# Fewer unread matmuls before chunk 0, and batch 2's first transposes at the end of chunk 0

## The chip, the cores and the metric

The kernel runs on one core of one Trainium2 chip (trn2). The core has five engines that follow their own instruction streams: TensorE (PE in the profile; its weight loads are PEld), VectorE (DVE), ScalarE (ACT), GpSimd (POOL) and SyncE (SP). The metric is the device time in microseconds (us), as the median of several executions. For the kernel before it is 323.74 us, the median of five (322.66 to 325.79).

## The reference

Two layers follow each other: sliding-window causal attention over 64 positions, and a mixer whose token mixing is of low rank, followed by an MLP.

```python
# q, k, v: (8, 8, 576, 64)
scores = scale * np.matmul(q, k.transpose(0, 1, 3, 2))
mask = (rel >= 0) & (rel < 64)            # rel = query position - key position
attn = softmax(np.where(mask, scores, -1e9))
x = np.matmul(attn, v)                    # heads side by side: (8, 576, 512)
h = x.transpose(0, 2, 1) @ U @ V          # U (576, 32), V (32, 576)
u = x + h.transpose(0, 2, 1)
out = u + np.maximum(u @ w_ch1, 0.0) @ w_ch2   # 512 -> 2048 -> 512
```

## The kernel before

The 8 x 576 = 4608 tokens of the MLP are cut into nine chunks of 512 (`NCH`). A chunk needs attention and token mixing of its tokens first. A batch has 576 tokens, so chunk c of the MLP runs beside the attention of batch b = c + 1. Batch 0's attention stands alone in front of chunk 0.

The order of the work is written out by hand. `mlp(c)` gives a list of pieces that feed TensorE: 16 pieces `ch1(i)` (each four matmuls of 128x512 into a PSUM tile `psA`, L602, then a relu to `c1_i` on ScalarE, L613, or VectorE, L611) and 16 pieces `ch2(t, r)` (four matmuls into `psU`, L644; after the fourth quarter VectorE adds `u`, L653, into `osb`, which SP writes out). In chunk 0 the second half is ordered so that t = 0, 1, 2 advance together and t = 3 comes last. These 32 pieces are slots 0 to 31. The attention's pieces are put into slots by tables: `PLACE_1` for batch 1, `PLACE_2` for batch 2, `PLACE` for the later ones. A slot runs its MLP piece and then the pieces placed there; in chunk 0 after slot 20 the placed pieces come first. Instructions of one engine run in the order in which they are recorded.

The pieces of a batch are:

- `KT` (four for batches 0 to 2): VectorE transposes the raw keys and queries, L239, in the order keys 0, queries 0, keys 1, queries 1. They write `kt` and `qt`, of which there is one each. The raw data come by GpSimd's DMAs, `load_kq` (L105 for batches 0 to 2, L114 later); values by `load_v`, L126 and L130.
- `S` (six): scores in PSUM (`sc`, L345; for batch 0 L286 and L303), ScalarE's exp to `pts` (L353), and VectorE's product with the mask (L360). For a paired batch, the first two of the six need only keys 0 and queries 0.
- `VC`: copies of the values, shifted by 64 rows (L138, L139).
- `PV` (five): weights times values into `xr` (L382), the reciprocal of the row sums (L391) and the scaled result `xs` (L401).
- `U`, then `V` (three): token mixing. `V` makes `psv` (L453) and VectorE adds it to `xs`, giving `un` (L464), two tiles at a time. For batches 0 and 1, `XT` (L498) and `UP` (L512) make the transposed `uTc` directly in PSUM, which is copied out at L521.

PSUM tiles of two kinds matter here: the pool `ps_big` has two buffers, which `sc`, `xr`, `psv`, `xT` of batch 1 and the unread tiles take in turn; the pool `ps_mm` has three, which `psA` and `psU` take in turn.

`turn_over(n, cols)` (L698) issues n matmuls on a tile of zeros, whose results nobody reads. They keep TensorE busy while it has nothing else: 56 of 128 columns and 50 of 64 before batch 0's first scores, ten of 64 between its second and third score piece, one of 128 before and after its PV piece 3, and a few more before chunk 0. Each of them is two instructions, a weight load and a matmul.

For chunk 1 the tables give: slot 0 has `V` of batch 1 (first pair of tiles) and the transposes of keys 0 and queries 0 of batch 2, slot 1 the second pair of `V`, slot 2 keys 1, slot 3 queries 1 and the first two score pieces, slot 6 the next two, slot 8 the last two, slot 11 the first two PV pieces.

Of the kernel before, what the change touches and what calls it, by code (L numbers as in the profile page):

```python
# [16 lines left out]
def kernel(  # L17
# [12 lines left out]
    B, H, S, D = q.shape  # L30
# [3 lines left out]
    P = nc.NUM_PARTITIONS  # L34
    W = 64
# [63 lines left out]
    def load_kq(b):  # L99
        r = RUN[b]  # L100
        for part in range(NJ if PAIRED[b] else 4):
            for x, src in (("k", k), ("q", q)):
                dst = raw[x, b % 2]
                if PAIRED[b]:
                    nc.gpsimd.dma_start(  # L105
                        out=dst[:, part * RD : (part + 1) * RD],
                        in_=src[b, part * NQ : (part + 1) * NQ].rearrange(
                            "i (p c) d -> (i p) (c d)", c=RP
                        ),
                    )  # L110
                    continue
                m, dh = divmod(part, 2)
                off = 32 * (1 - dh)
                nc.gpsimd.dma_start(  # L114
                    out=dst[32 * part : 32 * (part + 1), off : off + NJJ * RD].rearrange(
                        "p (n x) -> p n x", x=r * D
                    ),
                    in_=src[b, m * NJJ : (m + 1) * NJJ].rearrange(
                        "h (m p e) d -> p (h m) (e d)", p=32, e=r
                    ),  # L120
                )

    def load_v(b):
        va, vb = vA[b % 2], vB[b % 2]
        for t in range(NFULL):
            nc.gpsimd.dma_start(  # L126
                out=va[:, t, :, 0:D],
                in_=v[b, :, t * P : (t + 1) * P, :].rearrange("h p d -> p h d"),
            )
        nc.gpsimd.dma_start(  # L130
            out=vb[0:W, NFULL, :, 0:D],
            in_=v[b, :, NFULL * P : S, :].rearrange("h p d -> p h d"),
        )
# [401 lines left out]
    def TR(g):  # L535
        def f():
            c, t = divmod(g, TPC)
            if c not in stages:
                stages[c] = stg_pool.tile([P, 4 * NDC, TPC, 32], BF16, name="stg")
            nc.vector.transpose(  # L540
                out=stages[c][:, :, t, :],
                in_=u_tiles[g].rearrange("p (j x) -> p j x", x=32),
            )

        return f

    def next_loads(c):
        def f():
            for i, j in last_pieces[c + 1]:
                rows = slice(32 * j, 32 * (j + 1))  # L550
                nc.gpsimd.tensor_copy(
                    out=hold[rows, 0:1], in_=uT_of(c + 1)[rows, 0, i * TPC * 32 : i * TPC * 32 + 1]
                )
            load_kq(c + 3)

        return f

    def gather(c):
        def f():
            run = TPC * 32  # L560
            queues = (nc.sync, nc.scalar, nc.gpsimd)
            done = {}
            for n in range(16):
                i, j = (n + n // 4) % 4, n % 4
                done[n % 3] = (i, j)
                queues[n % 3].dma_start(  # L566
                    out=uT_of(c)[32 * j : 32 * (j + 1), :, i * run : (i + 1) * run],
                    in_=stages[c][32 * i : 32 * (i + 1)].rearrange(
                        "p (d j) t q -> p d j (t q)", j=4
                    )[:, :, j, :],  # L570
                )
            last_pieces[c] = (done[0], done[1])

        return f

        return f

    def mlp(c):
# [102 lines left out]
    }  # L681
    PLACE_2 = {
        "V1": [0, 1, 17],
        "KT": [0, 0, 2, 3],
        "S": [3, 3, 6, 6, 8, 8],
        "VC": [7],
        "PV": [11, 11, 13, 13, 15],
        "U": [16],
        "V": [18, 19, 21],
    }  # L690
# [7 lines left out]
    def turn_over(n, cols=CH, to=None):  # L698
        for _ in range(n):
            nc.tensor.matmul(  # L700
                (unread if to is None else to)[:, 0, 0:cols],
                idle[:, 0:P],
                idle[:, 0:cols],
                start=to is None,
                stop=to is None,
            )

    def fresh():
        return ps_big.tile([P, 2, CH], FP32, name="unread", tag="big")

    unread = fresh()
    turn_over(56, P)
    turn_over(50, W)
    att = {0: attention(0, alone=True)}
    a = att[0]
    for f in a["KT"]:
        f()
    a["S"][0]()
    a["S"][1]()
    turn_over(10, W)  # L720
    a["S"][2]()
    for f in a["VC"][0:2]:
        f()
# [16 lines left out]
    xT0 = [psum["x0"].tile([P, 2, CH], FP32, name=f"xT{i}", tag="x0") for i in range(2)]  # L740
    unread = xT0[0]
    a["PV"][2]()
    turn_over(1, P)
    a["PV"][3]()
    turn_over(1, P)
    a["PV"][4]()
    a["XT"][0]()
    turn_over(2, P, xT0[0])
# [17 lines left out]
    for c in range(NCH):  # L766
        slots = [[] for _ in range(NSLOT + 1)]

        def place(b, parts, where):
            if b not in att:  # L770
                att[b] = attention(b)
            for part in parts:
                for f, s in zip(att[b][part], where[part]):
                    slots[s].append(f)

        b = c + 1
        if b == 1:
            for f, n in zip(att[0]["V"], (6, 8, 10)):
                slots[n].append(f)
        if b < B:  # L780
            if b == 1:
                load_kq(2)
            if b + 1 < B:
                load_v(b + 1)
            if b == 1:
                slots[23].append(lambda: load_kq(3))
            where = {1: PLACE_1, 2: PLACE_2}.get(b, PLACE)
            if b == 2:
                place(1, ("V",), {"V": where["V1"]})
            if b <= 2:  # L790
                place(b, ("KT",), where)
            place(b, ("VC", "S", "PV"), where)
            if 3 <= b + 1 < B:
                place(b + 1, ("KT",), {"KT": KT_LATE[b]} if b in KT_LATE else PLACE)
            place(b, ("U", "XT", "UP") if b == 1 else ("U", "V"), where)
        if 2 <= c + 1 < NCH:
            g0 = (b * S) // P
            first = (c + 1) * TPC
            last = max(first + t - g0 for t in range(TPC)) // 2 if b < B else 0
            ready = where["V"][last] if b < B else 18  # L800
            for t in range(TPC):
                slots[ready - 1 + t // 2 if t < TPC - 1 else ready + 1].append(TR(first + t))
            slots[ready + 1].append(gather(c + 1))
            if c > 0 and c + 3 < B:
                slots[ready + 1].append(next_loads(c))
        for n, (fill, extra) in enumerate(zip(mlp(c) + [lambda: None], slots)):
            early = c == 0 and n > 20
            for f in extra + [fill] if early else [fill] + extra:
                f()
# [30 lines left out]
```

## Time and profile before

| what | value |
|---|---|
| median of five executions | 323.74 us (322.66 to 325.79) |
| the profiled execution: device time | 324.57 us |
| the profiled execution: span from first to last instruction | 322.9 us |
| mean granted TensorE clock | 0.982 of full speed |
| VectorE busy | 208.9 us |
| ScalarE busy | 106.9 us |
| L602 psA, 576 matmuls | 132.8 us, 380 ns each |
| L644 psU, 560 matmuls | 127.2 us, 379 ns each |
| chunk 0 begins (first psA) | 24.96 us |

How to read it: a line of a timeline gives the start, the duration, the engine, the line of the kernel, the operation, out<-in, the tile's shape, and how many were merged; brackets at the end give the idle time of the engine before it and what ended it. [...]512-column matmuls shown with 380 ns follow each other every 216 ns; distances are better taken from start to start. A line of the stretches gives, for a window, each engine's busy time with its count of instructions, then the granted TensorE clock, the DMA share (outstanding packets over 16 engines, so it can pass 1) and GB/s.

### The profile page before, as it was taken

What the parts mean: (1) busy time and instruction counts of PE and PEld (TensorE: products, weight loads), DVE (VectorE), ACT (ScalarE), POOL (GpSimd) and SP (SyncE); (2) the same over time, 40 slices, a digit from 0 to 9 for tenths busy, and PEclk for the clock granted to TensorE, in tenths of its full rate; (3) what the DMA queues carried; (4) which work ended last, traced back from release to release, by engine and by line L of the source; (5) the groups of instructions that cost most, each with busy time, mean ns of one, the idle gap of its engine ahead of it and who ended that gap; (6) DMA issues with size and microseconds to landing.
All of it is one profiled execution on the core that took longest, in us unless ns stands there. A gap on an engine that the chain in (4) does not pass through costs nothing.

```text
span 322.9 us, 7092 instructions
## 1 busy us (share of the span) xinstructions
PE 313.3 (97%) x2929; PEld 154.0 (48%) x2929; DVE 208.9 (65%) x366; ACT 106.9 (33%) x174; POOL 105.1 (33%) x156
## 2 busy tenths in 40 slices
PE   7799999989999999999999999999999999999995
PEld 7474454545444544454444444444444444444444
DVE  7544968478698759777957795879578722412211
ACT  1535363265205520552046303730273004203400
POOL 8672428541038403751394036512000200030000
PEclk9859999999999999999999999999999999999999
DMA  7999999999639993899999929995500150050011
GB/s 119 160 196 208 206 124 149 210 194 135 20 94 181 173 116 85 157 165 136 90 186 195 116 37 181 195 145 30 181 0 2 32 164 1 2 163 32 2 67 65
DMA packets 108929, 38.05 MB, mean 118 GB/s; under 512 B 98352, under 2 KB 101808, under 8 KB 108896
## 3 DMA queue, kind: packets, MB, share of 16 engines
q0 software_dynamic: 92480, 25.63, 107.1%
q1 hardware_dynamic: 11232, 10.69, 9.9%
q10 hardware_dynamic: 5184, 1.28, 1.8%
q8 instruction: 23, 0.38, 0.5%
q14 instruction: 10, 0.08, 0.1%
HBM read 48.94 MB, written 9.44 MB: 181 GB/s over the span
## 4 chain that ended last, share of the span: by engine, by line
PE 88%; DMA 6%; DVE 3%; issue 1%; POOL 0%; DVEq 0%; POOLq 0%
PE psU L644 37%; PE psA L602 36%; PE xr L382 4%; DMA vA<-in_v_dram 4%; PE sc L345 3%; DMA qr<-in_q_dram 2%; PE psv L453 2%; DVE un L464 1%; PE psU L626 1%; PE xT L498 1%; PE pshh L434 1%; PE xT L512 1%; PE sc L303 1%; DVE qt L239 1%; PE sc L286 1%
## 5 line engine op out<-in xcount | busy, mean ns | idle before, releaser
L602 PE MATMUL psA<-uTc,w1b 128*128 128x512 bf16 x576 | 132.8, 380 | 0.1
L644 PE MATMUL psU<-w2b,c 128*128 128x512 bf16 x560 | 127.2, 379 | 0.0
L613 ACT ACTIVATE c<-psA 128x512 bf16<-128x512 f32 x101 | 60.3, 597 | 171.0 <-PE psA L602 170.7
L644 PEld LDWEIGHTS <-c 128*128 128x128 bf16 x560 | 53.5, 98 | 63.9 <-issue 1.5
L602 PEld LDWEIGHTS <-w1b 128*128 128x128 bf16 x576 | 53.5, 98 | 61.7 <-issue 0.3
L566 POOL DMA_DIRECT2D uTc<-stg x35 | 19.2, 556 | 117.5 <-DVE stg L540 78.5
L653 DVE TENSOR_TENSOR osb<-psU,un 128x512 f32<-128x512 f32 x35 | 23.5, 671 | 33.6 <-PE psU L644 33.5
L611 DVE TENSOR_SCALAR c<-psA 128x512 bf16<-128x512 f32 x43 | 29.5, 687 | 22.4 <-PE psA L602 20.8
L126 POOL DMA_DIRECT2D vA<-in_v_dram x32 | 28.5, 893 | 28.2 <-PE psA L602 12.6
L360 DVE TENSOR_TENSOR pts<-pts,mask 128x768 bf16<-128x768 bf16 x42 | 22.8, 556 | 17.9 <-ACT pts L353 15.8
L353 ACT ACTIVATE pts<-sc 128x768 bf16<-128x768 f32 x42 | 31.8, 810 | 3.9 <-PE sc L345 3.9
L464 DVE TENSOR_TENSOR un<-psv,xs 128x512 bf16<-128x512 f32 (+1 forms) x40 | 26.0, 675 | 10.8 <-PE psv L453 10.6
L401 DVE TENSOR_TENSOR xs<-xr,rcp 128x512 bf16<-128x512 f32 (+1 forms) x39 | 26.9, 691 | 1.3
L382 PEld LDWEIGHTS <-pts 128*64 128x64 bf16 x576 | 13.4, 116 | 10.5 <-DVE xs L401 5.1
L540 DVE STREAM_TRANSPOSE stg<-un 128x512 bf16<-128x512 bf16 x28 | 18.4, 683 | 0.0
L114 POOL DMA_DIRECT2D kr<-in_k_dram x20 | 16.7, 837 | 3.6 <-DMA vA<-in_v_dram 2.1
L247 DVE STREAM_TRANSPOSE qt<-qr 128x576 bf16<-128x576 bf16 x20 | 15.8, 788 | 3.2 <-DMA vA<-in_v_dram 3.2
L114 POOL DMA_DIRECT2D qr<-in_q_dram x20 | 16.8, 841 | 1.8 <-DMA vA<-in_v_dram 1.0
L382 PE MATMUL xr<-vB,pts 128*64 128x65 bf16 x320 | 16.6, 202 | 0.2 <-issue 0.2
L247 DVE STREAM_TRANSPOSE kt<-kr 128x576 bf16<-128x576 bf16 x20 | 15.7, 786 | 1.2 <-DMA kr<-in_k_dram 1.2
L345 PEld LDWEIGHTS <-kt 64*64 64x64 bf16 (+1 forms) x720 | 10.2, 106 | 10.8 <-issue 9.1
L345 PE MATMUL sc<-qt,kt 64*64 64x128 bf16 (+4 forms) x720 | 13.3, 215 | 1.5 <-DVE qt L239 0.7
(70 smaller groups left out, 165.4 us busy)
## 6 DMA issues: line engine op xcount, KB each, us to landing
out_dram<-osb SPq DMA_DIRECT2D x35, 256.0 KB, 2.2
kr<-in_k_dram POOLq DMA_DIRECT2D x26, 288.0 KB, 10.8
qr<-in_q_dram POOLq DMA_DIRECT2D x26, 288.0 KB, 12.0
vA<-in_v_dram POOLq DMA_DIRECT2D x32, 128.0 KB, 13.3
w2b<-in_moe_w_ch_dram POOLq DMA_DIRECT2D x2, 1024.0 KB, 19.7
uTc<-stg SPq DMA_DIRECT2D x42, 32.0 KB, 2.3
uTc<-stg ACTq DMA_DIRECT2D x35, 32.0 KB, 2.3
uTc<-stg POOLq DMA_DIRECT2D x35, 32.0 KB, 2.0
```

The lines of the kernel that those rows point to most:

```text
L114: nc.gpsimd.dma_start(out=dst[32 * part : 32 * (part + 1), off : off + NJJ * RD].rearrange("p (n x) -> p n x", x=r * D), in_=src[b, m * NJ ...
L126: nc.gpsimd.dma_start(out=va[:, t, :, 0:D], in_=v[b, :, t * P : (t + 1) * P, :].rearrange("h p d -> p h d"),)
L247: nc.vector.transpose(out=dst[:, n * S : (n + 1) * S].rearrange("q (m p e) -> q m e p", p=32, e=r), in_=src[:, 32 + n * RD : 32 + (n + 1) ...
L345: nc.tensor.matmul(sc[half * W : (half + 1) * W, g, (a - lo) * W : (z - lo) * W], operand("k", g, jj, e, kb * W, (kb + 1) * W), operand("q ...
L353: nc.scalar.activation(out=dst, in_=sc[:, :, 0 : PB * W].rearrange("p g (n w) -> p g n w", w=W), func=ACT.Exp, scale=scale,)
L382: nc.tensor.matmul(xr[r0 : r0 + W, h // 4, (h % 4) * VW : (h % 4 + 1) * VW], pts[:, g, jj * NB + blk, :], rhs, start=True, stop=True,)
L401: nc.vector.tensor_tensor(out=x[lo:hi, t, :, :].rearrange("p (a h) d -> p a h d", a=2), in0=xv[:, :, :, 0:D], in1=rcp[lo:hi].to_broadcast( ...
L464: nc.vector.tensor_tensor(out=u_tiles[g][rs, :], in0=ps[rs, n, :], in1=xt[n][rs], op=ALU.add)
L602: nc.tensor.matmul(to if c < 2 else to.rearrange("p (t i q) -> p t i q", i=4, t=TPC), w1b[:, dc, n * P : (n + 1) * P], uT_cols(dc), start= ...
L611: nc.vector.tensor_relu(out=c1[i][:], in_=ps)
L613: nc.scalar.activation(out=c1[i][:], in_=ps, func=ACT.Relu)
L644: nc.tensor.matmul(acc[t][:], c1[i][:, t * P : (t + 1) * P], w2b[:, i, :], start=(i == 0), stop=(i == NFC - 1),)
```

## The change

It changes three things. The unread matmuls: 74 of 156 columns instead of 56 of 128 and 50 of 64 in front; two of 512 columns instead of ten of 64 between score pieces; the two single ones between PV pieces are dropped. Batch 2's transposes of keys 0 and queries 0 move from slot 0 of chunk 1 to slots 30 and 31 of chunk 0, where they stand ahead of those slots' MLP pieces. Batch 2's last two score pieces move from slot 8 to slot 9.

```diff
     PLACE_2 = {
         "V1": [0, 1, 17],
-        "KT": [0, 0, 2, 3],
-        "S": [3, 3, 6, 6, 8, 8],
+        "KT0": [30, 31],
+        "KT": [2, 3],
+        "S": [3, 3, 6, 6, 9, 9],
...
     unread = fresh()
-    turn_over(56, P)
-    turn_over(50, W)
+    turn_over(74, 156)
...
-    turn_over(10, W)
+    turn_over(2)
...
     a["PV"][2]()
-    turn_over(1, P)
     a["PV"][3]()
-    turn_over(1, P)
     a["PV"][4]()
...
-            if b <= 2:
-                place(b, ("KT",), where)
+            if b == 1:
+                place(1, ("KT",), where)
+            if b == 2:
+                att[2]["KT"] = att[2]["KT"][2:]
+                place(2, ("KT",), where)
             place(b, ("VC", "S", "PV"), where)
+            if b == 1:
+                place(2, ("KT",), {"KT": PLACE_2["KT0"]})
```

P is 128, W is 64, and `turn_over` without a width uses 512 columns.

## Prediction

> **What bounds the kernel now.** I read the page first: its engine shares, the clock row and the chain that ended last.
>
> ```profile
> PE 313.3 (97%) x2929; PEld 154.0 (48%) x2929; DVE 208.9 (65%) x366; ACT 106.9 (33%) x174; POOL 105.1 (33%) x156
> PEclk9859999999999999999999999999999999999999
> q8 instruction: 23, 0.38, 0.5%
> PE 88%; DMA 6%; DVE 3%; issue 1%; POOL 0%; DVEq 0%; POOLq 0%
> ```
>
> TensorE carries the span, and the chain is TensorE in nearly every stage. So only two things are worth anything: TensorE's own work, and the holes between its matmuls. After chunk 0 begins (24.96 us) the waits of TensorE list very few holes, so I went to its timeline for chunk 1:
>
> ```profile
> 40.12 0.76 PE L345 MATMUL sc<-qt,kt 32*64 32x128 bf16 x48
> 40.81 1.90 PE L644 MATMUL psU<-w2b,c 128*128 128x512 bf16 x8
> ...
> 64.05 1.89 PE L602 MATMUL psA<-uTc,w1b 128*128 128x512 bf16 x8
> 66.66 0.54 PE L345 MATMUL sc<-qt,kt 32*64 32x128 bf16 x24 [0.72 <-DVE qt L239]
> 67.77 0.54 PE L345 MATMUL sc<-qt,kt 32*64 32x128 bf16 x24 [0.57 <-DVE un L464]
> 68.25 2.76 PE L602 MATMUL psA<-uTc,w1b 128*128 128x512 bf16 x12
> 70.94 0.82 PE L345 MATMUL sc<-qt,kt 32*64 32x128 bf16 x56
> 71.69 1.90 PE L602 MATMUL psA<-uTc,w1b 128*128 128x512 bf16 x8
> 73.52 0.64 PE L345 MATMUL sc<-qt,kt 32*64 32x64 bf16 x43
> 74.41 0.37 PE L345 MATMUL sc<-qt,kt 32*64 32x128 bf16 x13 [0.24 <-issue]
> ```
>
> Three holes stand in ten microseconds. The first waits for a transpose of batch 2's queries, the second for VectorE to free a PSUM buffer (`un`, L464), and the third for nothing that the profile shows ("issue"). VectorE in the same stretch says why:
>
> ```profile
> 59.07 1.29 DVE L521 CAST uTc<-xT 128x512 bf16<-128x512 f32 x2 [2.91 <-PE xT L512]
> 61.66 0.69 DVE L653 TENSOR_TENSOR osb<-psU,un 128x512 f32<-128x512 f32 x1 [1.30 <-PE psU L644]
> 62.96 1.40 DVE L464 TENSOR_TENSOR un<-psv,xs 64x512 bf16<-64x512 f32 x2 [0.60 <-PE psv L453]
> 64.27 1.25 DVE L239 STREAM_TRANSPOSE kt<-kr 128x576 uint32<-128x576 uint32 x1
> 65.36 1.24 DVE L239 STREAM_TRANSPOSE qt<-qr 128x576 uint32<-128x576 uint32 x1
> 66.44 1.28 DVE L464 TENSOR_TENSOR un<-psv,xs 128x512 bf16<-128x512 f32 x2
> ```
>
> It is idle for 1.30 and 0.60 us before chunk 1, and then has six things to do in a row while TensorE waits for the fourth and the last.
>
> **Part 1: two transposes to the end of chunk 0.** I measure by starts[...]. Eight psA matmuls followed by scores take 73.52 - 71.69 = 1.83 us, so the first scores could start at 64.05 + 1.83 = 65.88. A pair of score pieces of 48 matmuls needs 40.81 - 40.12 = 0.69 us, so psA could go on at 66.57. It goes on at 68.25. The two holes cost 1.68 us.
>
> Where do the two transposes go? After the casts of L521, in the idle stretch. With the pitches of the rows (1.20 for a pair of L521 or L464, 1.09 and 1.08 for the transposes, 0.6 for osb): casts 59.07 to 60.27, kt from there, qt from 61.36 (ends 62.6), osb at 62.44 instead of 61.66, the first `un` pair at 63.1, the second at 64.4, ended 65.7. Their raw data landed long before: the last packets of the two loads of L105 (issued 45.86 and 47.18) at 50.85 and 52.22. They write the single kt and qt tiles, whose last readers, batch 1's scores, are through at 46.9.
>
> What is queued behind them? The osb add, 0.8 us later, frees the psU bank that chunk 1's third psA piece takes (start 64.05): freed at 63.1, 0.9 us to spare. Its output DMA on SP goes as much later, with three more osb buffers and nobody waiting. The second `un` pair frees the buffer for the second score piece: 65.7 against 65.88 + 0.35 = 66.2, 0.5 us to spare. The other two transposes then run 65.6 to 67.9, and the next score piece needs them at 66.57 + 2.69 = 69.3. No DMA is moved, and POOL's queue is not passed. So this part gives **-1.68**; the cover that makes the move free is VectorE's idle time of 1.9 us, and without it the two transposes (2.2 us) would only change places.
>
> **Part 2: last scores one piece later (8 to 9).** The same 56 matmuls, so no work on TensorE. But ScalarE now has c_9's relu ahead of their exps. With the rows' exps (0.75 each in a pair) and mask products (0.6), the last product ends about 75.4 while TensorE reaches the second PV piece, its reader, at about 75.5 (77.47 + 0.32 less 1.68 and the 0.44 of part 3). In before 0.7 us lay between. Bounds: 0 and 0.3. I take **+0.1**.
>
> **Part 3: 42 fewer unread matmuls.** I counted TensorE's instructions in the built program and paired them one to one with the trace's 2929 weight loads and 2929 matmuls. Two stalls with the "issue" mark are true stalls: at 18.91 us, instruction 706, and at 74.41, instruction 1986. They are 1280 = 5 x 256 apart. So I read 706 + 256k as the block borders. The trace's records of the instruction queue (the page's q8, 23 packets of 16 KB) fit: packets landed at 17.37 and 72.80, and TensorE went on 1.54 and 1.61 us later. The second stall costs (74.71 - 73.52) - (71.69 - 70.94) = 0.44 us.
>
> Here a rule speaks against the change. The Trainium skill, "Runtime: NRT & Kernel Launch", section "Instruction fetch mechanics", says that instructions come in blocks of 256, fetched ahead, and that the cost of a border is "mostly hidden". By the rule, moving borders is worth 0 and the whole change gives -1.6; by the row it is worth up to 0.44 at each of two borders. The rows decide: at 20 of 22 borders the rule holds, and at two, where the block before is full of short matmuls, it fails.
>
> The change takes out 84 instructions (118 unread matmuls become 76, each with a weight load), so the borders fall on old instructions 790 + 256k. The border at 18.91 moves to the UP matmuls (0.2 to 0.4 us each, 22.7 to 24.4), where the block has 3 us more. Its stall was worth little: the next PV piece waits until 18.93 for `xs` of PV 2 (VectorE, ended 18.90) anyhow. Without the stall and the two unread matmuls between PV pieces, I get that piece at about 19.0 instead of 19.33. But the last U matmul follows the last `xs` (21.00, matmul 21.07), and VectorE's chain of rcp 0.24 and xs 0.69 ends that one only 0.24 earlier. The granted clock there is half:
>
> ```profile
> 14.00:14.50 0.50, 0.50 (x31) 0.49 (x32) 0.00 (x0) 0.50 (x1) 0.32 (x1) 0.67 1.81 173
> 24.00:24.50 0.50, 0.50 (x4) 0.23 (x3) 0.00 (x0) 0.30 (x1) 0.12 (x1) 0.59 1.08 205
> ```
>
> It falls near 14.17 and returns near 24.41, by the clock and not by the work, so 0.24 gained before is filled with half-speed matmuls: **-0.12** (between 0 and -0.35).
>
> The border at 74.41 moves to the start of the second PV piece, and the one before it to old instruction 1814, in the middle of the third and fourth score pieces: 71.2 less 1.68 = 69.5. From there to the new border at about 75.7 is 6.2 us. How long does a block need from the crossing of the border before? Crossing 14.01, usable 18.91: 4.9 us. Crossing 67.97, usable 74.41: 6.4 us. The next packet (asked for at 74.41) landed at 81.59, so usable about 83.1: 8.7 us. The DMA share rises from 1.83 to 2.57 and 4.31 in those stretches (68 to 72, 72 to 76, 76 to 80). Bounds for the new stall: 0 and 2.5. The nearest row is the second, 1.5 us earlier in the kernel: 6.4 - 6.2 = 0.2; with the rising load I take 0.3. So this border gives -0.44 + 0.3 = **-0.14**.
>
> The warm-up itself is free: 74 matmuls of 156 columns, 130 ns each until 3.93 us and 67 after (from 107 and 56 ns at 128 columns), end at 7.55 instead of 7.11, and the first scores wait for qt until 8.45. The two of 512 columns (0.43 for 0.29) lie before the wait until 12.22 for the second qt, whose data comes by DMA.
>
> **Sum.** -1.68 + 0.1 - 0.12 - 0.14 = -1.84, made against the profiled execution: 324.57 (span 322.9 and 1.7 around it) becomes 322.7. That execution lies 0.83 above the median of the five, 323.74, which becomes 321.9. Later stages keep the gain: the loads of L114 and L126 follow TensorE's progress (POOL waits for psA), and batch 3's raw data landed by 80.1 with its first transpose at 92.12.
>
> **Rivals.**
> *The block arrives late (slower).* The fetch asked for at 69.5 meets batch 2 and 3's loads as the one of 74.41 did, takes 8.7 us or a little more, and TensorE stops 2.5 us or more before the second PV piece. From a fetch of 8.3 us on (6.2 + 2.14, all other gains) the kernel is slower. For it: the DMA share of 4.31. Against: the fetch of 67.97 lies nearer. Time: 323.74 - 2.14 + 2.6 = 324.2. Chance 0.10.
> *The gain is not passed on.* A later wait stands at a fixed time. For it: a hole of 0.37 at 188.18, behind loads that took 13.07 us. Against: those loads start on TensorE's progress. It would leave stage 0 and a part: 323.3. Chance 0.13.
> *The clock moves.* "TensorE: Matmul & The Clock Gate", section "Part 1: The HAM clock gate", says that the clock falls only after an idle window of about 3.4 us[...]; the trace differs, it fell after a hole of 1.62 us (10.6 to 12.22). By the rule the change's denser filler gives 0. By the row the start is near a limit. If the half clock did not come, 16 matmuls of XT and 4 of UP would save 16 x 51 + 4 x 210 ns = 1.7 us, with the rest some 2.5: 319.4. Chance 0.07. Longer half speed into chunk 0 would cost half of its length; it shares the slow side's remainder.
> *The likeliest*, 0.70: 320.9 to 322.9 by itself.
>
> **How the numbers follow.** A measurement of this kernel can tell about 0.5% (1.6 us) from no change. The forecast 321.9 is 0.57% below 323.74, hence close to that line: of its 0.70 some 0.43 lies below 322.1, 0.24 within, and 0.03 is left for a longer half speed (slower); clock 0.07 faster; not passed on 0.13 same; late block 0.05 within, 0.05 slower. So faster 0.50, same 0.42, slower 0.08. The range 320.5 to 323.7 leaves out the clock case and most of the late block.
>
> **What would show it.** Right: the first two score pieces of chunk 1 start near 65.9 and 66.2 and psA follows at 66.6, without the marks of qt and un; the transposes stand at 60.3 and 61.4 on VectorE with osb behind them; no issue mark inside a score pair of chunk 1. Wrong: a new hole of TensorE at 62 to 65 (osb's bank), an issue mark of over 0.5 us at the second PV piece near 75.7, PV waiting for the mask product, or other times at which the clock falls and returns; these would void parts 1, 3, 2 and the sum's base in turn.

## The result and the profile after

The changed kernel takes 322.91 us as the median of 43 executions, the kernel before 324.56 us as the median of 80 in the same measurements (its first five had 323.74). These medians lie 1.65 us apart. The ratio on record leaves out slow executions, those over 1.5% above the fastest of the same kernel (five of the changed kernel's): it is 0.9934 with a 95% interval of 0.9918 to 0.9950, 0.66% or 2.1 us faster. The forecast ratio was 0.9943. The profiled execution has 323.18 us with a span of 321.5, against 324.57 and 322.9, so that pair shows 1.4 us.

From the page of the changed kernel:

```profile
PE 313.0 (97%) x2887; PEld 154.4 (48%) x2887; DVE 208.6 (65%) x366; ACT 106.7 (33%) x174; POOL 104.5 (33%) x156
PEclk9959999999999999999999999999999999999999
PE 58%; DMA 22%; DVE 7%; POOL 5%; issue 4%; SPq 3%; ACT 1%; DVEq 0%; POOLq 0%; ACTq 0%
```

TensorE is as busy as before. The chain's shares look very different, but that is no new bound: it is followed back from the end through whatever released each step, and where it now takes the loads, those themselves start on TensorE's progress. Chunks 2 to 8 have the same lengths as before within 0.6 us. TensorE's timeline shows what did move:

```profile
14.29 0.19 PE L382 MATMUL xr<-vB,pts 128*64 128x65 bf16 x1
15.54 0.19 PE L382 MATMUL xr<-vA,pts 128*64 128x65 bf16 x1 [1.06 <-issue]
...
45.67 0.75 PE L345 MATMUL sc<-qt,kt 32*64 32x64 bf16 x51
47.05 0.25 PE L345 MATMUL sc<-qt,kt 32*64 32x128 bf16 x5 [0.64 <-issue]
47.23 1.04 PE L644 MATMUL psU<-w2b,c 128*128 128x512 bf16 x4
...
64.49 1.89 PE L602 MATMUL psA<-uTc,w1b 128*128 128x512 bf16 x8
66.31 0.76 PE L345 MATMUL sc<-qt,kt 32*64 32x128 bf16 x48
67.00 2.76 PE L602 MATMUL psA<-uTc,w1b 128*128 128x512 bf16 x12
69.69 0.82 PE L345 MATMUL sc<-qt,kt 32*64 32x128 bf16 x56
70.44 2.76 PE L602 MATMUL psA<-uTc,w1b 128*128 128x512 bf16 x12
73.13 0.79 PE L345 MATMUL sc<-qt,kt 32*64 32x64 bf16 x56
```

In chunk 1 all three holes are closed: from the psA matmuls at 64.49 to those at 67.00 are 2.51 us, where before 68.25 - 64.05 = 4.20 were needed. But two "issue" stalls stand at places that had none before: 1.06 us in batch 0's first PV piece, and 0.64 us inside batch 1's last score pair in chunk 0, which before ran through:

```profile
46.09 0.78 PE L345 MATMUL sc<-qt,kt 32*64 32x64 bf16 x56
46.80 1.04 PE L644 MATMUL psU<-w2b,c 128*128 128x512 bf16 x4
```

VectorE after the change, in the stretch of the moved transposes:

```profile
59.51 1.29 DVE L521 CAST uTc<-xT 128x512 bf16<-128x512 f32 x2 [2.91 <-PE xT L512]
60.71 1.25 DVE L239 STREAM_TRANSPOSE kt<-kr 128x576 uint32<-128x576 uint32 x1
61.80 1.24 DVE L239 STREAM_TRANSPOSE qt<-qr 128x576 uint32<-128x576 uint32 x1
62.88 0.68 DVE L653 TENSOR_TENSOR osb<-psU,un 128x512 f32<-128x512 f32 x1
63.60 2.59 DVE L464 TENSOR_TENSOR un<-psv,xs 64x512 bf16<-64x512 f32 x4
```

They fill the idle time, the add waits for them, and the four `un` follow without a break. TensorE shows no wait for the late osb.

By stages, measured between the first psA weight loads of the chunks in the profiled executions (us; the kernels in the lower rows are those of the experiments below):

| kernel | first stage | chunk 0 | chunk 1 | chunks 2 to 6 | ratio to before (95%) |
|---|---|---|---|---|---|
| before | 24.91 | 36.34 | 36.92 | 165.5 | 1 |
| changed | 24.50 | 37.19 | 34.77 | 165.9 | 0.9934 (0.9918 to 0.9950) |
| place_only | 24.41 | 36.34 | 34.77 | 165.4 | 0.9926 (0.9896 to 0.9955) |
| kt_only | 27.09 | 36.80 | 34.88 | 165.0 | 0.9949 (0.9928 to 0.9969) |
| spread_only | 25.49 | 36.34 | 36.45 | 164.7 | 0.9968 (0.9946 to 0.9990) |
| unread_only | 25.80 | 37.16 | 37.44 | 164.7 | 0.9998 (0.9973 to 1.0023) |
| borders_back | 23.78 | 36.34 | 34.76 | 164.9 | 0.9908 (0.9876 to 0.9940) |
| borders_s56 | 24.44 | 36.35 | 34.77 | 165.0 | 0.9893 (0.9858 to 0.9929) |
| plus_256 | 25.19 | 37.34 | 34.77 | 164.7 | 0.9996 (0.9971 to 1.0021) |

The first stage differs from execution to execution of one kernel, so its column is one draw. Chunks 0 and 1 repeat to a tenth in these rows except where TensorE stalls at a border of the instruction blocks. Such a stall is no constant of a border either: kt_only has one of 0.28 us in chunk 0 (at 48.67), at a border that before and place_only cross without a wait.

### The profile page after: what moved, and what is told of

The parts are those of the page before. It is cut to its first block, busy times and chain, and to the rows that moved or that the text cites. A ratio compares the mean times of both kernels' runs of the same rounds, so it can differ in the third digit from the quotient of the medians.

```text
span 321.5 us, 7008 instructions
## 1 busy us (share of the span) xinstructions
PE 313.0 (97%) x2887; PEld 154.4 (48%) x2887; DVE 208.6 (65%) x366; ACT 106.7 (33%) x174; POOL 104.5 (33%) x156
## 4 chain that ended last, share of the span: by engine, by line
PE 58%; DMA 22%; DVE 7%; POOL 5%; issue 4%; SPq 3%; ACT 1%; DVEq 0%; POOLq 0%; ACTq 0%
PE psA L602 24%; PE psU L644 24%; DMA qr<-in_q_dram 10%; DMA vA<-in_v_dram 8%; SPq L566 3%; PE xr L382 3%; DMA vB<-in_v_dram 2%; POOL kr L114 2%; DMA uTc<-stg 2%; PE sc L345 2%; POOL qr L114 2%; DVE un L464 2%; PE psv L453 1%; DVE stg L540 1%; PE psU L626 1%
## 5 line engine op out<-in xcount | busy, mean ns | idle before, releaser
L382 PE MATMUL xr<-vA,pts 128*64 128x65 bf16 x256 | 13.0, 200 | 1.1 <-issue 1.1
```

Source lines behind the costliest of these rows:

```text
L382: nc.tensor.matmul(xr[r0 : r0 + W, h // 4, (h % 4) * VW : (h % 4 + 1) * VW], pts[:, g, jj * NB + blk, :], rhs, start=True, stop=True,)
```

## The experiments

**Moving batch 2's pieces alone** (place_only): the diff of `PLACE_2` and of the placing, with the unread matmuls of before.

> Only batch 2's transposes and last scores are moved; the unread matmuls and so the instruction blocks stay as before. Theory 1 (two holes of 1.68 us in chunk 1 go, blocks move stalls about): 1.6 us less than before (0.5 less than 2.0 more than 1.2), psA after the first score pair 2.5 us after the psA pieces of slots 2 and 3 began (3 to 4.2 before), and the stall of some 0.4 us in the last score pair of chunk 1 still there. Rival, the clock: the gain comes from the wider unread matmuls keeping the clock up, and this gives 0. Rival, the borders: the holes hid the fetch of a block, and closing them only lengthens the stall in the last score pair to 1 us or more: 0.9 less.

Measured 0.9926: the whole gain of the change. Chunk 1 is 2.15 us shorter, not 1.7, since the stall inside the last score pair went too. The rival of the clock falls, since the unread matmuls are those of before. Theory 1 was wrong about that stall.

**Changing the unread matmuls alone** (unread_only).

> Only the unread matmuls are changed; batch 2's pieces stay where they were. Theory 1: the holes of 0.7 and 0.6 us at batch 2's first scores stay; stalls stand at the new borders, about 1.1 us in batch 0's first PV piece and 0.6 us in batch 1's last score pair, those of 0.4 us at the old borders are gone; on balance within 0.7 us of before. Rival, the clock: 2 us less, with a shorter or absent stretch at half clock. Rival, the borders: 0.4 to 0.9 less.

Measured 0.9998. Its trace has the new stalls at 17.21 (2.72 us) and 48.32, and the old holes:

```profile
48.32 0.25 PE L345 MATMUL sc<-qt,kt 32*64 32x128 bf16 x5 [0.60 <-issue]
...
68.37 0.54 PE L345 MATMUL sc<-qt,kt 32*64 32x128 bf16 x24 [0.71 <-DVE qt L239]
69.48 0.54 PE L345 MATMUL sc<-qt,kt 32*64 32x128 bf16 x24 [0.57 <-DVE un L464]
```

There is a third stall of 0.78 us at the second PV piece of chunk 1 (79.89), the place that the prediction named. So this part of the change gives nothing by itself that the interval (some 0.8 us each way) could show: what it wins at two borders it pays at others.

**Putting the borders back** (borders_back): as many columns in front, in 84 more instructions.

```diff
-    turn_over(74, 156)
+    turn_over(116, 100)
```

> The changed kernel with 116 unread matmuls of 100 columns in front instead of 74 of 156: as many columns, 84 instructions more, so each block border falls on the piece of work that it fell on before the change. Theory 1: the stalls in batch 0's first PV piece (1.1 us) and batch 1's last score pair (0.64 us) are gone, those in batch 0's PV piece 3 or 4 and in chunk 1's last score pair (0.4 us each) are back; 2.2 us less than before, about the changed kernel or 0.3 better. Rival, the clock: as the changed kernel. Rival, the borders (the change's own choice of border is what pays): 0.7 us slower than the changed kernel.

Measured 0.9908 (0.9876 to 0.9940). The time is on the side of theory 1, but its interval holds the changed kernel's 0.9934 too; it is the trace that speaks. The stalls at 15.5 and 47 are gone and chunk 0 is back at 36.34; one stands where the border now is:

```profile
16.66 0.19 PE L382 MATMUL xr<-vB,pts 128*64 128x65 bf16 x1
18.87 0.21 PE L382 MATMUL xr<-vA,pts 128*64 128x65 bf16 x1 [2.02 <-issue]
```

It is 2.02 us, not 0.4: here TensorE ran at full clock up to that place and came there earlier, while the block came when it came. The stall in chunk 1's last score pair did not return.

**A whole block more** (plus_256): 202 unread matmuls of 57 columns, so all borders fall on the same work as in the changed kernel.

> The changed kernel with 202 unread matmuls of 57 columns in front instead of 74 of 156: 256 instructions more, so the borders fall on the same work as in the changed kernel. Theory (place modulo 256 decides): stalls at the same two pieces, batch 0's first PV piece (1 to 2.5 us) and batch 1's last score pair (0.6 us), chunk 0 37.2 us; the time of the changed kernel within 0.7. Rival (how many unread matmuls stand in front decides, not where the borders fall): stalls elsewhere or none, chunk 0 36.3 us.

Both stalls stand at the pieces that the theory names, for instance

```profile
46.36 0.75 PE L345 MATMUL sc<-qt,kt 32*64 32x64 bf16 x51
47.90 0.25 PE L345 MATMUL sc<-qt,kt 32*64 32x128 bf16 x5 [0.79 <-issue]
```

but the time missed: 0.9996, with a median 1.7 us above the changed kernel's. A third stall, 1.84 us before the scores' matmuls at 11.15, is at the place where the changed kernel crosses a border without one. Here one more border lies before it, crossed at 5.58, and TensorE is through with that block at 9.1. But the stalls of this trace do not explain the 1.7 us. The traced execution is the fastest of the 14 (322.83 us, mean clock 0.995) and no slower than the changed kernel's traced one (323.18). Eight of the 14 have a mean clock of 0.979 or less, against 0.983 at the least in the changed kernel, and take 324.6 us in the mean, so a longer stretch at half clock goes with it. Why it comes is open.

**Each half of the moved pieces** (kt_only moves the transposes, spread_only the last scores).

> The kernel before with only the two transposes moved to the end of chunk 0; batch 2's last scores stay at slot 8, the unread matmuls stay. Theory (a fetch needs about 6 us from border to border): both holes at batch 2's first scores go, 1.68 us; but the borders at instructions 1730 and 1986 then lie 5.9 us apart, so the stall inside the last score pair of chunk 1 stays or grows to 0.4 to 1 us. Chunk 1 takes 35.2 to 35.6 us (36.92 before, 34.77 with the scores spread too), 1.4 us less than before in all. Rival (the spread of the scores is idle): chunk 1 takes 34.8 us, no stall.

> The kernel before with only batch 2's last scores moved from slot 8 to slot 9. Theory: the two holes of 0.7 and 0.6 us stay; four psA matmuls more lie between the borders 1730 and 1986, 0.86 us, so the stall of 0.44 us in the last score pair goes. Chunk 1 takes 36.5 us, 0.4 less than before. Rival (the spread is idle): 36.9, as before, with the stall still there.

kt_only: 0.9949, chunk 1 34.88 us; the stall that I expected in its last score pair shrank to 0.1, so here the rival was right. spread_only: 0.9968 (0.9946 to 0.9990), chunk 1 36.45, as expected:

```profile
67.23 0.54 PE L345 MATMUL sc<-qt,kt 32*64 32x128 bf16 x24 [0.72 <-DVE qt L239]
68.35 0.54 PE L345 MATMUL sc<-qt,kt 32*64 32x128 bf16 x24 [0.57 <-DVE un L464]
...
74.96 0.78 PE L345 MATMUL sc<-qt,kt 32*64 32x64 bf16 x56
```

The holes are there, the stall in the last pair (74.41 in before) is not. The stall of 0.44 is thus removed by either half: the spread puts four psA matmuls between the two borders (6.75 us from crossing to crossing). With the transposes moved the distance was hardly longer, 6.06 us against 5.98 up to the stall in before, but the block landed 4.45 us after the crossing instead of 4.83. Why it came sooner is not shown.

**A better place for the borders** (borders_s56, and again as s56_again), chosen by the time between borders in the changed kernel's trace.

```diff
-    turn_over(74, 156)
+    turn_over(46, 251)
```

> The changed kernel with 46 unread matmuls of 251 columns in front: as many columns, 56 instructions fewer, so each border falls 56 instructions later in the work. By the time between borders in the changed kernel's trace, with its two stalls taken out: 4.8 us into the border near 15.2, 6.6 into that near 47.8, over 7.2 at all others, against 6 needed. Theory 1: one stall of 0.6 to 1.2 us before 16 us, none at 47 and none in chunk 1; 0.5 us less than the changed kernel, 2.6 less than before. Rival, the clock: as the changed kernel.

> The kernel of borders_s56 once more (46 unread matmuls of 251 columns in front), to see whether it beats the changed kernel. Theory (borders decide): a ratio to before of 0.988 to 0.992, chunk 0 36.35 us and chunk 1 34.77 with no stall, one stall of 1 to 2 us in batch 0's score pieces. Rival (its first result was a lucky draw of the first stage): 0.993 to 0.996.

Measured 0.9893 and 0.9911 (0.9881 to 0.9941): some 0.2 to 0.4% below the changed kernel's 0.9934, though the intervals overlap, so that it is faster is not shown. Chunk 0 lost its stall (36.35 us; 36.73 in the second trace, without a stall at a border), and the only one left is in the first stage, 1.56 us before 16.84 and 0.31 before 16.04.

**What the unread columns buy** (short_front cuts the changed kernel's 74 to 16 columns, s56_short the 46 of borders_s56).

> The changed kernel with its 74 unread matmuls cut from 156 columns to 16, so that TensorE has some 2 us instead of 7 in front of the first scores; instructions and borders as in the changed kernel. Theory 1 (the columns only matter for the clock, and chunk 1 carries the gain): the clock rises later or falls earlier, the first stage ends 0.5 to 3 us later, chunk 1 still takes 34.8 us; 1 to 3 us slower than the changed kernel. Rival, the clock is set by later work alone: as the changed kernel within 0.5.

> The same with the 46 unread matmuls cut to 16 columns: borders as there, but hardly any time spent on unread matmuls in front. Theory (in the first stage the loads and the fetch of the blocks set the end, not the clock): as s56_again within 0.8 us, although the clock is at half until some 20 to 25 us. Rival (short_front was saved by its block stall, which hid the slow clock; here there is less to hide behind): 1.5 us or more slower than s56_again.

short_front: 0.9918 (0.9885 to 0.9952), no slower than the changed kernel, so theory 1 missed there. Its matmuls do run at half speed nearly to the end of the first stage: twelve of 128 columns take 23.84 - 22.59 = 1.25 us, 104 ns each.

```profile
22.59 1.46 PE L498 MATMUL xT<-ident,xs 128*128 128x128 bf16 x12
23.84 1.66 PE L512 MATMUL xT<-vrep,hh 128*128 128x512 bf16 x4
```

With half the clock the stall in the first PV piece is gone: the block landed at 13.72, and TensorE comes to the border at 16.40. s56_short: 0.9940 (0.9915 to 0.9964), by the medians 1.4 us above s56_again, by the ratios 0.9: between the theory and the rival. One reading is that the seven microseconds of unread matmuls pay only where the border does not take the time back; in both pairs the intervals overlap, so it is not shown.

**Filling the wait before the third score piece** (s56_fill).

```diff
-    turn_over(46, 251)
+    turn_over(43, 268)
...
-    turn_over(2)
+    turn_over(5)
```

> borders_s56 with three of its unread matmuls moved: 43 of 268 columns in front, and five instead of two of 512 columns between batch 0's second and third score piece, where TensorE otherwise waits 0.4 to 1.0 us for the second transposed queries. Borders fall as there. Theory (the wait of about 1 us lets the clock fall): the half clock comes less often, 0.5 us less than borders_s56, ratio to before 0.987 to 0.990. Rival (the stall at the block border and the short matmuls let it fall anyway): as borders_s56, 0.989 to 0.991.

Measured 0.9926 (0.9893 to 0.9959), no gain. The wait for qt was gone, but the clock fell all the same at 16.65, and the stall at the border before 17.62 had 2.08 us. My theory of the wait as the cause of the fall is not supported.

## Why the prediction was right, and which of its terms were not

**Part 1, the transposes: right.** -1.68 was forecast for the two holes; 4.20 - 2.51 = 1.69 was measured, and kt_only shows the same with nothing else changed: 69.21 - 66.69 = 2.52. VectorE's order and its spare times came as worked out, with everything 0.4 us later.

**Part 2, the spread: wrong sign.** "I take +0.1" for PV's wait on the mask product: TensorE shows no such wait, chunk 1 has 34.77. The spread gave slack at a border instead (spread_only: -0.47 in chunk 1).

**Part 3, the borders: the mechanism was right, the accounting was not.** The borders lie at 706 + 256k: every stall with the "issue" mark in the first 90 us of all these traces, waits of up to 0.22 us apart, is at such a place, to the instruction or the one beside it. The forecast stall of 0.3 at the second PV piece did not come in the changed kernel (the block had landed 2.50 us earlier), and came with 0.78 in unread_only. But the step "at 20 of 22 borders the rule holds" took all other borders as harmless wherever they went. Two were not: 1.06 us of idle time at the first PV piece (1.25 from start to start), and 0.64 in chunk 0, which made that chunk 37.19 - 36.34 = 0.85 us longer. The prediction's own yardstick, 4.9 and 6.4 us from one crossing to the next block's use, points at both: in the changed kernel's trace TensorE took 4.8 us from 9.49 to the stalled place at 14.29, and 5.8 us from 40.39 to that at 46.20. Forecast for part 3: -0.26. Measured for it alone: ratio 0.9998, that is about 0.

"The warm-up itself is free" came out by another way. In the changed kernel's trace the unread matmuls came 130 ns apart until 6.6 us, not 3.9, so the next matmul started at 8.83 (7.55 was forecast) and the first scores at 9.25 instead of 8.45. The third score piece, which waits for qt, came at 11.87 all the same (12.22 before).

**The sum.** Forecast -1.84 on one profiled execution; the pair shows -0.4 in the first stage, +0.85 in chunk 0, -2.15 in chunk 1 and +0.3 later, together -1.4; all executions show -1.65 by the medians and -2.1 by the ratio. That the number came so near is luck in part, for errors of parts 2 and 3 cancelled in part: 0.4 us too little from chunk 1, 0.85 too little charged to chunk 0. The range held the time; the absolute forecast of 321.9 stood on a median of five that was 0.8 us low.

**The first stage.** "By the clock and not by the work" was read from one execution, and its times are no constants: the clock fell at 14.17 in before, at 16.86 in the changed kernel, at 20.21 in place_only, and not at all in s56_again's profile. It stayed at half for 10.24, 6.83 and 3.41 us: whole multiples of the window of about 3.4 us that the Trainium skill gives in "TensorE: Matmul & The Clock Gate", section "Part 1: The HAM clock gate". That a whole such window must be idle before it falls does not fit: no hole of TensorE after 8 us in the changed kernel is longer than 1.06.

**The rivals.** The late block was the right kind of fear in the wrong place. The moving clock is not what the gain rests on: place_only leaves the unread matmuls as they were and has all of it, and unread_only changes them and gains nothing that shows. But the case came true in single executions. By the mean clocks on record, 9 of the changed kernel's 44 (the profiled one counted) and 5 of unread_only's 14 have 0.998 or more, which leaves no room for a fall to half like those above, while with the unread matmuls of before (before, place_only, kt_only, spread_only) no execution has more than 0.995. In the changed kernel these nine are the fastest, 320.6 us in the mean against 323.2 for the others, so it is no slow start that such a mean hides (see the end). The new unread matmuls do seem to keep the clock up at times, which is worth 0.5 us on the mean of all 44. Since unread_only as a whole gains nothing, about as much is lost again; its trace shows stalls at borders that could take it.

**Open.** From one border's crossing to the use of a block at a stalled border 4.3 us (place_only, 14.54 to 18.81) to 8.7 us (unread_only, 8.55 to 17.22) pass, and I can't say what sets it. In the changed kernel the fetch for the border in chunk 0 began 3.9 us after the crossing of the one before (40.39), in before 2.2 us after (40.15), though TensorE needed about as long from the crossing to the border (5.8 and 6.0 us). The work in front of the crossing could set it, or the loads in flight; no run separates them.

## What to carry to other kernels

When TensorE sets the time, look for its holes by distances between starts, and ask what the other engine could have done in its own idle time just before; 1.7 us came from moving two instructions into such time. When a change moves the number of TensorE's instructions, lay all block borders against the work, not only those that stall now, and compare the time between neighbouring borders with what passed here from a crossing to the next block's use, mostly some 6 us (4.3 to 8.7). A fix of one border by shifting the rest is a lottery unless that list is made, and even with it the stalls differ from one execution to another.

## What was not expected of the hardware

A fetched block became usable only 1.3 to 2.0 us after its 16 KB packet had landed, at every stalled border (17.37 to 18.91 and 72.80 to 74.41 before; 13.56 to 15.54 and 45.63 to 47.05 after). "Runtime: NRT & Kernel Launch", section "Instruction fetch mechanics", calls a border's cost mostly hidden; here that holds at the borders behind long matmuls, and fails by up to 2.9 us (spread_only, before 20.45) at some of those behind 256 instructions that are mostly short ones.

The mean granted clock of short_front is given as 1.000, although its matmuls run at half up to 25 us: the record holds changes only, and there the first change is the rise at 25.1. So a high mean clock is no proof of a fast start; the matmuls' spacing is.
